# Deltanet then MLP-mixer on one core: 1999 steps of a hand-kept order of work permuted

## The chip, the cores and the metric

The kernel runs on one core of a Trainium2 chip. The core has five engines with an instruction queue each: TensorE (PE in the profile, its weight loads apart as PEld), VectorE (DVE), ScalarE (ACT), GpSimd (POOL) and SyncE (SP), which here issues every transfer between HBM and the core's memory. The metric is device time in microseconds (us), lower is better. Times are medians of several executions; one execution is taken with the hardware profiler and gives the profile and the trace.

## The reference

Two blocks follow one another. The first is a linear-attention recurrence (delta rule) over 768 tokens for 4 batch items of 8 heads of 48 elements; the second an MLP-mixer with a token part (768 to 256 to 768) and a channel part (384 to 1536 to 384), which takes the first block's output with the heads side by side.

```python
k_n = k / (np.linalg.norm(k, axis=-1, keepdims=True) + 1e-06)
for t in range(S):
    kt, vt, bt = (k_n[:, :, t], v[:, :, t], beta[:, :, t, None])
    y[:, :, t] = np.einsum('bhd,bhde->bhe', q[:, :, t], state)
    v_old = np.einsum('bhde,bhd->bhe', state, kt)
    state = state + bt[:, :, :, None] * np.einsum('bhd,bhe->bhde', kt, vt - v_old)
...
xt = x.transpose(0, 2, 1)
h = np.maximum(xt @ w_tok1, 0.0) @ w_tok2
u = x + h.transpose(0, 2, 1)
h2 = np.maximum(u @ w_ch1, 0.0) @ w_ch2
return (u + h2).astype(np.float32)
```

## The kernel before, in words

**Chunks, units, batches.** The recurrence is done in chunks of 64 tokens: 12 chunks to a batch item, 48 in all (`recur`, r0 to r47). What a chunk needs besides the state is made ahead for a unit of two chunks (128 tokens of one batch item, all 8 heads; u0 to u23): its k and q rows, their turned form, the products of k and q within a chunk, and the inverse of a triangular matrix for each head. When the 12 chunks of a batch item are through, its mixer (m0 to m3) can run.

**Jobs.** Each piece of work is a Python generator, and each `yield` in it ends a step. The jobs, named by a letter and a number:
- `k` loads k and q (L385). From unit 12 on, `load_rows` (L359) brings the k rows in four transfers into a tile called `pads`, `stacked` (L403) brings k once more into `kst`, and `load_rows` brings the q rows in four.
- `p` (prep) turns the rows with VectorE transposes (`turn_rows`, L368) and makes norms and scales. `c` and `d` (`grams`) are the products within the unit's two chunks: matmuls into `p_g` (L442), then a VectorE product with a mask into `gm` (L445).
- `t` (`to_parts`, L612) writes 32-row blocks of `gm` to a buffer in HBM called `n_dram`; `i` (`invert`) reads the blocks of several units as one tile `x` and inverts them on VectorE in a round of some thirty steps, each a product into `sub` (L676) and an addition to `x` (L680); `f` (`from_parts`, L637) brings the blocks back from `w_dram`. The first two rounds (units 0 to 5) stay on the chip and need no such transfers; round 2 holds units 6 to 9, round 4 units 14 to 17, round 5 units 18 to 21. `h` and `j` (`join_16`, `join`) put larger inverses together from the blocks.
- `v` loads v of a unit into `v_st` (four transfers, L403) and scales it on GpSimd (L416).
- `r` is a chunk of the recurrence: matmuls with the state (L813), the subtraction of `v_st` (L820), two more groups of products, the new state `s_t` (VectorE, L860) and the output rows, copied into `xb`, the mixer's input.
- `m` is a mixer. Its token part has the products `p` (L1009) and `p_h` (L1022); `p_h` is added into `xb` by VectorE (L1026), six times. Then the rows are turned on PE (transposes, copied by ScalarE at L1036 into `u_t`), and the channel part follows for pairs of 128 tokens: `p_c` (L1089) in the first mixer, a scheme with fewer products (L981 to L997) in the others, combinations on VectorE (L1063), and seven products `p_o` (L1111), each added into `xb` by VectorE (L1040).
- `w` rounds the mixer's weights from 64-bit input (ScalarE, VectorE at L282, GpSimd at L286) and makes differences of some (VectorE, L301); `s` makes weight sums (VectorE, L922); `b` loads beta. `x`, `z`, `y` and `Y` are filler matmuls on zeros (L227, L237), which only keep PE at work.

**PSUM.** The mixer's products share three PSUM banks (L101, `bufs=3`), taken in turn: the fourth group has to wait until the first group's bank has been read. Two banks each serve the recurrence and the preparation.

**The order of the work.** `manual_schedule` is on, so nothing reorders instructions: each engine runs its instructions in the order in which the program issues them, and waits where a semaphore says so. That order is a table at the end of the kernel function, a string of 2740 steps. A loop takes the words one after another and moves the named job on by one step:

```python
for word in order.split():
    name, _, n = word.partition("*")
    for _ in range(int(n or 1)):
        next(jobs[name])
```

`k13*4 r14` thus issues four steps of unit 13's load (here four transfers on SP) and then one step of chunk 14. One step can put instructions on several queues.

Of the kernel before, what the change touches and what calls it, by code (L numbers as in the profile page):

```python
# [23 lines left out]
def kernel(  # L24
# [149 lines left out]
    t11 = const.tile([128, NB, HB], FP32, name="t11")  # L174
# [18 lines left out]
    w1 = const.tile([128, NCH, DTOK], FP32, name="w1")  # L193
# [998 lines left out]
    p6 w8 v0 i0*2 k8 p4 i0 w1 i0*2 p6 p4*3 c4 w1 i0 w17 w1 c4*4 x i0*2 p5 z k7 w8
    k8 i0*2 z i0 k8 w6 k8 i0*3 x z v1 z k8 z d4 x d4 w17 d4 w6 d4 z h0 d4 w17 t4
    h0*4 i0 h1 w0 f0 k8 h1 f0 p6 h1 p3 h1 f0 h1 z w8 k7 f1*3 h0*4 h2*2 h0*4 k7*2
    h2*2 v1 h2 p5 w8 w11 w0 z f2 j0 f2 j0*5 w0 h1*2 f2 h1*3 j0 h1 v0 h1*2 w6 j0*3
    p5 j1 p5*2 t4 p5 w0 h2 j0 p5 h2 p5*3 h2*2 r0*2 w6 h2 r0*2 h2*2 r0 h2 c5*4 w14
    r0*2 d5 w11 d5*2 c5 w11*2 r0 r1*4 w14 d5 r1 d5 p6 t5 r1 j1*3 r1 k9 j1 w9 r1 k7
    p6 k10 h3*3 w14 t5*2 j1*2 h3 p8 j1 j2 j1*2 r1 r2*3 t4 i1 r2 r1 i1 h3 j2 f3*2 x
    r2 j1 w9 p6 v2*4 w16 w14 j2 v2 f3 j2 k9 r2 i1 k9 r2 p8 j2 p6 i1 j2 i1 r2 p7
    h3*2 r2 p6 r2 h3 d6 k9*3 h3 p6 d6 i1*2 d6*2 r3*2 k7 w27 h3*2 r3*2 h3*2 p8 k10  # L1200
    c6 i1 w9 c6 r3*2 c6 w9 k10 w16 d6 i1 v3 c6 w16 r3 j2 k10 j2 r3 c6 j2 j3 r3
    r4*2 j2 v3 r4 p7 r4 p8 j3 w16 i1 r3 p7 j3 v3 j3 t6 r4 j3 j2 i1 p9 w24 p7 r4*2
    j3 p7*2 k10 i1 r4 p7 v3 p7*2 w5 r4 p7 t6*2 r4 r5*4 i1 c7 w27 r5 d7 c7 v4 i1 c7
    d7 k11 c7 r5 v3 i1 r5 d7 c7 d7 v4 w5 r5 d7 p8 j3 r5 p8 w5 w24 j3 r6*2 i1 w27
    w5 r6*2 p8 j3*2 w24 p9 w27 p8 r6 p8 t7 x z h5*3 w26 t7 j3 h5 r5 h4 t7 v4 t7 h4
    r6 w24 i1 t6 h5 p9 h4*2 r6 c8*2 h4 v4 w28 r6 c8 f4*2 p9 d8 c8 r6 w7 c8 f4 d8*4
    h4 r7*2 h4*2 r6 r7*2 w26 h4*2 w26 r7 h4 p9 v4 h4 t8 j4 h4 w26 p9 r7 t8 p9*2
    r7*3 p9 w28 c9*2 d9 c9 f5 c9 r8*2 d9 r8 w28 d9 c9 t8 f5*2 w7 d9 j4 w4 d9 w28
    w27 t8 p8 v5 r8 v5 p10 j4*3 m0 j4 p10 j4 w27 j4*2 w7 p10 w15 j4 r7 h5 r8 j4 w4
    t9*2 h5*2 w27 p10 h5 r8 w4 r8 z t9 w7 r8 w15 h5*2 w15 t9 r8 r9 h5 p9 k10 v5 r8  # L1210
    r9*2 w4 j5 r9*2 h5 p10 v5 w15 i2 r9 j5*2 p10 r9*2 w19 r9 v5 Y j5 i2*4 p10 j5 x
    j5 r10 i2 j5*2 r10 w29 p10*2 r9 k12 i2 Y i2 r10*2 j5 k12 j5 k11 w12 r10 k11
    k12 k11*2 z j5 w19 Y c10 r10 i2 Y i2*2 r10*2 w29 k12 w12 d10 w29 i2 d10 m0
    k12*2 r10 i2 k12 r11 w12 k12 r11*2 c10 r11 i2 d10 p11 r10 k11 w12 r11 w22 x*2
    p11 w29 i2 v6 i2 w19 k12 w19 i2 z w22 i2 v6*2 m0 k12 i2 v7*2 r11 w22 r11 v6
    w22 w25 m0*2 w21 k12*2 c10 r11 d10 r11 c10 p12 p11 m0 i2*6 m0 w31 i2 m0 i2*4
    w21 i2*2 v7 w25 w31 m0*2 f6 c10 m0*2 f6*2 p11 w31 m0 w31 m0 f6 f7*3 s p12 w21
    f7 p11 s d10 v6 p11 p10 j6 p12 w25 f8*2 m0 w25 f8*2 w21 m0*2 j6*3 p12 j6*2 m0
    j7*6 j8 m0 r12*5 w23*2 w20 j8 w29 j8 r12 v7 f9 j8 w25 f9*2 r12 j8 r13*2 r12
    r13 w30 j8 p11 w23 s r13 t10*2 r13 w23 p12 v8 m0 v8 k13 w32 r13 p11 r13*3 k13  # L1220
    p11 c11 w23 c11 k13 w20 d11 w30 w29 c11 v8 d11 c11 w20 c11 w30 v7 d11 r14 t10
    r13 w25 w32 d11 r14 w30 r14 j9 d11 k13*4 r14 w20 p12 k13 p12 r14 m0 w32 m0*2
    k13*2 m0 k13 r14 c12 w32 r14 t11 d12 v8 c12 d12 c12 p11 p13 t11 d12*2 r14 k13
    r14 d12 p12 m0 r15 v8 c12 p13*2 r15*4 m0 c12 t10 w33 r14 r15 f9 p13 t12 p13*3
    m0 t11 m0*2 d13 t12 t11 c13 r15 d13 c13 t12 d13 c13 d13 k14*2 w33*2 c13 r15*2
    d13 c13 m0 k14 m0 k14*2 w33 k14*2 s w31 w33 m0 w23 r16 k14 t13 j9 r16 t13*2 j9
    r16 j9 r16 w33 t12 r16 w29 j9 r15 m0*2 t13 j9 w31 r16 w31 v9 m0 p14*2 r16 w23
    r16 k14*2 r16 m0 r17 w25 i3 j9 w33 r17 p14 j9 p13 k14 v9 r17 j9 p14 r17 p14
    r17 v10 k15*3 v10 r16 m0*2 i3*3 k15 m0*3 k15 i3 v10 k14 k15 r17 i3 v9*2 r17
    i3*4 k15 i3 m0 p14 i3*2 r17*3 m0*2 p14 k15 i3*2 m0*2 v9 p14 m0*2 i3*4 m0 i3*2  # L1230
    k15*2 r18 d14 k15 r18*2 p15 d14 r18*2 j9 m0 i3 k15 i3 p15 i3*2 j9 p15 i3*7
# [36 lines left out]
    j18 t23 m1 j19*4 i6 m1 j19 f21*2 m1*4 r36*4 m1 r35 i6*4 m1 j20 m1 f19 f20 i6
    r36 i6 r36 i6 r36 i6 m2*2 i6*2 m1 r37*3 r36 r37 i6 r37 i6 m2*3 i6 r37*2 v19*3
# [48 lines left out]
```

## Time and profile before

| | before |
|---|---|
| median of 3 runs | 646.3 us |
| the runs | 644.84, 646.3, 648.53 us |
| profiled execution | 642.82 us |
| its span on the core | 641.0 us |
| mean granted TensorE clock | 0.987 |
| bytes read from / written to HBM | 39.42 / 9.44 MB |

The profiled execution is 3.5 us below the median of the runs and 2.0 below the fastest. Its span is the time from the first to the last instruction; some 1.8 us lie around it. In the tables by stage, a stretch has the busy time of PE, PEld, DVE, ACT and POOL with the count of instructions in brackets, then the granted TensorE clock, the mean busy share of the DMA engines and GB/s. In a timeline row stand the start, the duration, the engine, the line, the operation, the tile written and the tiles read, the count, and in square brackets the idle time of that engine just before with what ended it. SPq is SP's queue: its rows are the issues of transfers, not the transfers themselves.

### The profile page before, as it was taken

The page shows a single profiled execution, that of the slowest core. Times are in us where ns is not written, and L with a number is a line of the kernel's source. Part 1 is how long each engine was busy: PE and PEld are TensorE (multiplying, and loading weights), DVE is VectorE, ACT ScalarE, POOL GpSimd, SP SyncE. Part 2 cuts the span into 40 slices and gives each one's busy share as a digit, 9 for nine tenths or more (in the row PEclk, how much of TensorE's full clock was granted, in tenths as well). Part 3 has the DMA queues.
Part 4 walks back from the last instruction along what each step waited for, and adds up shares of the span by engine and source line. Part 5 has one row for each costly group of instructions (what it writes and reads, how often), then busy time and mean ns, then how long its engine had stood idle before and what let it go on. Part 6 is the DMA issues. An engine that isn't in the chain of part 4 may idle for free.

```text
span 641.0 us, 21509 instructions
## 1 busy us (share of the span) xinstructions
PE 613.8 (96%) x9136; PEld 531.7 (83%) x9136; DVE 443.0 (69%) x1132; ACT 260.4 (41%) x631; POOL 108.9 (17%) x147
## 2 busy tenths in 40 slices
PE   7499899999999999999989999999999999999997
PEld 4358786568898988959989999769999987999997
DVE  4885877987879568987958998784727253373643
ACT  7749787446413232125513424044334131132240
POOL 2446354243310122021121001000100000000000
PEclk9889899999999999999989999999999999999999
DMA  9785667546552454244442223203010000000000
GB/s 170 164 173 123 146 156 199 140 96 155 112 127 60 82 114 102 67 119 80 96 100 69 63 69 55 59 7 56 4 41 2 27 2 0 26 1 26 2 26 26
DMA packets 135776, 50.27 MB, mean 78 GB/s; under 512 B 114656, under 2 KB 130144, under 8 KB 135680
## 3 DMA queue, kind: packets, MB, share of 16 engines
q1 hardware_dynamic: 135680, 48.89, 34.3%
q8 instruction: 72, 1.18, 0.8%
q14 instruction: 24, 0.20, 0.1%
HBM read 39.42 MB, written 9.44 MB: 76 GB/s over the span
## 4 chain that ended last, share of the span: by engine, by line
PE 79%; DVE 7%; ACT 5%; DMA 3%; SPq 3%; issue 2%; POOL 0%; DVEq 0%; ACTq 0%; POOLq 0%
PE p_o L1111 25%; PE p_r L981 19%; PE p_c L1089 7%; PE p_h L1022 4%; PE p L1009 4%; PE p_g L442 3%; PE p_k L813 2%; PE p_s L851 2%; PE p_y L833 2%; PE p_z L773 2%; DVE sub L676 2%; SPq L403 2%; DVE x L680 2%; PE p_warm L227 2%; PE p_w L837 1%
## 5 line engine op out<-in xcount | busy, mean ns | idle before, releaser
L1111 PE MATMUL p_o<-wc,r 128*128 128x192 f32 x720 | 128.7, 331 | 0.6 <-ACT u_t L1036 0.6
L1111 PEld LDWEIGHTS p_o<-wc,r 128*128 128x128 f32 x720 | 117.6, 191 | 3.0 <-ACT u_t L1036 1.1
L993 DVE TENSOR_TENSOR r<-r,p_r 128x512 f32<-128x512 f32 x90 | 60.0, 685 | 49.0 <-PE p_r L981 48.1
L990 ACT COPY r<-p_r 128x512 f32<-128x512 f32 x54 | 31.6, 585 | 94.2 <-PE p_r L981 87.2
L1040 DVE TENSOR_TENSOR xb<-xb,p_o 128x192 f32<-128x192 f32 x84 | 29.4, 350 | 57.1 <-PE p_o L1111 56.7
L680 DVE TENSOR_TENSOR x<-x,sub 128x84 f32<-128x84 f32 (+24 forms) x178 | 61.2, 344 | 6.1
L676 DVE TENSOR_TENSOR sub<-x 128x84 f32<-128x84 f32 (+24 forms) x178 | 57.8, 325 | 5.8 <-DMA x<-n_dram 1.9
L416 POOL TENSOR_TENSOR v_st<-v_st,nrm 128x384 f32<-128x384 f32 x24 | 20.8, 866 | 180.2 <-DMA v_st<-in_v_dram 134.0
L1111 PE MATMUL p_o<-wc,s 128*128 128x192 f32 x288 | 50.7, 330 | 0.3 <-DVE xb L1040 0.3
L1089 PE MATMUL p_c<-u_t,wc 128*128 128x256 f32 x216 | 50.5, 386 | 0.2 <-ACT u_t L1036 0.2
L442 PE MATMUL p_g<-kq 48*64 48x128 f32 (+1 forms) x704 | 38.9, 284 | 12.3 <-ACT kq L511 9.1
L1111 PEld LDWEIGHTS p_o<-wc,s 128*128 128x128 f32 x288 | 46.7, 190 | 1.2 <-DVE xb L1040 0.6
L997 ACT ACTIVATE r<-r 128x512 f32<-128x512 f32 x54 | 33.8, 630 | 28.5 <-DVE r L993 28.2
L1089 PEld LDWEIGHTS p_c<-u_t,wc 128*128 128x128 f32 x216 | 39.9, 190 | 5.9 <-ACT u_t L1036 0.4
L865 ACT ACTIVATE xb<-p_y 64x192 f32<-64x192 f32 x96 | 31.2, 325 | 26.0 <-DMA out_dram<-xb 9.5
L442 PEld LDWEIGHTS p_g<-kq 48*64 48x64 f32 (+1 forms) x704 | 27.8, 136 | 16.4 <-ACT kq L511 11.0
L843 ACT COPY w_t<-p_w 128x192 f32<-128x192 f32 x48 | 15.2, 317 | 61.6 <-PE p_w L837 60.4
L981 PE MATMUL p_r<-u_t,wc 128*128 128x128 f32 x288 | 38.5, 277 | 0.0
L499 POOL TENSOR_TENSOR mb<-mask_c,cs 128x512 f32<-128x512 f32 x20 | 21.0, 1049 | 99.0 <-DVE gm L445 72.2
L981 PE MATMUL p_r<-t_d,wc 128*128 128x128 f32 x288 | 37.4, 280 | 0.0
L981 PEld LDWEIGHTS p_r<-u_t,wc 128*128 128x128 f32 x288 | 35.4, 192 | 0.3
L286 POOL TENSOR_TENSOR wc<-w_f,d 128x384 uint32<-128x384 uint32 x24 | 25.2, 1057 | 59.3 <-DVE w_f L282 28.8
(176 smaller groups left out, 1252.7 us busy)
## 6 DMA issues: line engine op xcount, KB each, us to landing
d<-in_moe_w_ch_dram SPq DMA_DIRECT2D x24, 384.0 KB, 3.8
v_st<-in_v_dram SPq DMA_DIRECT2D x96, 48.0 KB, 2.4
out_dram<-xb SPq DMA_DIRECT2D x23, 192.0 KB, 1.9
kst<-in_k_dram SPq DMA_DIRECT2D x64, 48.0 KB, 2.7
n_dram<-gm SPq DMA_DIRECT2D x72, 32.0 KB, 2.0
pads<-in_k_dram SPq DMA_DIRECT2D x24, 96.0 KB, 3.1
pads<-in_q_dram SPq DMA_DIRECT2D x24, 96.0 KB, 2.5
gm<-w_dram SPq DMA_DIRECT2D x72, 32.0 KB, 2.0
```

What stands on the lines that cost most here:

```text
L442: nc.tensor.matmul(p_g[PAR[i ^ cc], p], kqt[f, p, cc, 0], kqt[f, p, cc])
L676: nc.vector.tensor_tensor(out=tmp, in0=col.to_broadcast(dims), in1=row.to_broadcast(dims), op=ALU.mult,)
L680: nc.vector.tensor_tensor(out=new, in0=new, in1=tmp, op=ALU.add)
L865: nc.scalar.mul(y[:, :, D * i : D * i + D], p_y[PAR[1 - i]], 1.0 if c else -1.0)
L981: nc.tensor.matmul(p[:, i], pieces[i // width][:, at : at + 128], f[f"u{n}"], start=first and i == 0, stop=True, skip_group_check=True,)
L990: nc.scalar.copy(o, p)
L993: nc.vector.tensor_tensor(out=o, in0=o, in1=p, op=ALU.add if sign > 0 else ALU.subtract)
L997: nc.scalar.activation(o, o, ACTF.Relu)
L1009: nc.tensor.matmul(p_1[dh], piece_of(w1, c, 0)[:, dh * 128 : (dh + 1) * 128], xb[:, c], start=(c == 0), stop=(c == NCH - 1),)
L1040: nc.vector.tensor_tensor(out=xb[:, c, e], in0=xb[:, c, e], in1=p, op=ALU.add)
L1089: nc.tensor.matmul(p_c[:, k], piece_of(wc1, cb, f * 128)[:, f * 128 : (f + 1) * 128], u_t[:, cb], start=(cb == 0), stop=(cb == NCB - 1),)
L1111: nc.tensor.matmul(p, a[:, m], wc2[:, m, j], start=(start and i == 0), stop=(i == NM - 1), skip_group_check=True,)
```

## The change

The diff has one hunk: the table. Its first 1999 steps stand in another order; each step occurs as often as before, the fillers too, and each job's own steps keep their order. The last 741 steps are the same. No instruction is added, removed or altered, no tile or buffer has another size. Places that change hands between jobs (PSUM banks, buffers) are taken in the new order.

```diff
-    z*4 w10*3 k1 k0 w10 b k0 k1*5 p1*2 k0*3 k3 k0 b p0 w2 p1 k2 b v1 p0*4 x k2 k3
...
+    z*4 w10*4 x k1 k0 b k1*3 k0 k1*2 k0 p1 k0*2 p1 b w2 k0 p0*2 p1 v0 b p0 v0 p0*2
...
```

What it does is seen in the queues of the engines. Three places follow, in the order in which the prediction takes them up.

SyncE's queue where unit 21's q rows are loaded (about 320 us in the trace). `pads_92<-in_q_dram` are those rows, in four transfers; `v_st_4871` (before) and `v_st_4884` (after) are the v rows of unit 16; `n_dram` takes blocks to round 5 of the inversion, and `w_dram` is where blocks of round 4 come back from. Before:

```order
L403 DMA kst1_94<-in_k_dram 64x4x48 x4
L359 DMA pads_92<-in_q_dram 32x4x192
L359 DMA pads_92<-in_q_dram 32x4x160
L359 DMA pads_92<-in_q_dram 32x4x192
L612 DMA n_dram_4732<-gm_96 32x8x32
L403 DMA v_st_4871<-in_v_dram 64x4x48 x2
L612 DMA n_dram_4732<-gm_96 32x8x32 x2
L359 DMA pads_92<-in_q_dram 32x4x160
L637 DMA gm_96<-w_dram_4419 32x8x32
```

After:

```order
L403 DMA kst1_94<-in_k_dram 64x4x48 x3
L359 DMA pads_92<-in_q_dram 32x4x192
L359 DMA pads_92<-in_q_dram 32x4x160
L359 DMA pads_92<-in_q_dram 32x4x192
L359 DMA pads_92<-in_q_dram 32x4x160
L612 DMA n_dram_4812<-gm_96 32x8x32 x4
L637 DMA gm_96<-w_dram_4408 32x8x32
L612 DMA n_dram_4812<-gm_96 32x8x32
L637 DMA gm_96<-w_dram_4408 32x8x32
L612 DMA n_dram_4812<-gm_96 32x8x32 x2
L637 DMA gm_96<-w_dram_4408 32x8x32
L359 DMA pads_92<-in_k_dram 32x4x192
```

The fourth q transfer has moved up behind the third, ahead of the three `n_dram` and two `v_st` transfers; the two `v_st` transfers stand three rows further down than the last row shown, behind the first k rows of unit 22 and two more `n_dram` transfers.

VectorE's queue where the first mixer adds its token products (about 129 us). The rows of L676 and L680 are steps of round 2 of the inversion, counted by the last number of the x row (24x7, 25x6 and so on); L1026 are the adds that free the mixer's banks. Before:

```order
L676 TENSOR_TENSOR sub<-x 128x168
L680 TENSOR_TENSOR x<-x,sub 128x24x7
L1026 TENSOR_TENSOR xb<-xb,p_h 128x384
L676 TENSOR_TENSOR sub<-x 128x150
L680 TENSOR_TENSOR x<-x,sub 128x25x6
L1026 TENSOR_TENSOR xb<-xb,p_h 128x384
L676 TENSOR_TENSOR sub<-x 128x130
L680 TENSOR_TENSOR x<-x,sub 128x26x5
L676 TENSOR_TENSOR sub<-x 128x108
L680 TENSOR_TENSOR x<-x,sub 128x27x4
```

After:

```order
L676 TENSOR_TENSOR sub<-x 128x150
L680 TENSOR_TENSOR x<-x,sub 128x25x6
L676 TENSOR_TENSOR sub<-x 128x130
L680 TENSOR_TENSOR x<-x,sub 128x26x5
L676 TENSOR_TENSOR sub<-x 128x108
L680 TENSOR_TENSOR x<-x,sub 128x27x4
L1026 TENSOR_TENSOR xb<-xb,p_h 128x384
L676 TENSOR_TENSOR sub<-x 128x84
L680 TENSOR_TENSOR x<-x,sub 128x28x3
L1026 TENSOR_TENSOR xb<-xb,p_h 128x384
```

The first two adds stand three steps of the inversion later. A mask product `gm<-p_g,mb` (L445), which before stood behind the fourth add, now stands eight steps ahead of the first, behind the step 19x12.

VectorE's queue in the first mixer's channel part (about 170 us). L1063 are combinations for the products, L1040 is the add that frees a bank, L301 are weight differences, L922 a weight sum. Before:

```order
L368 STREAM_TRANSPOSE kq_99<-pads 128x4x4x32 x2
L1063 TENSOR_TENSOR s_2721<-r_2411 128x384
L1063 TENSOR_TENSOR s_2722<-s_2721,r_2411 128x384
L1063 TENSOR_TENSOR r_2411<-r_2411 128x3x128
L282 TENSOR_SCALAR w_f<-d_2833 128x384
L860 TENSOR_TENSOR s_t_113<-s_t_114,p_s 128x192
L445 TENSOR_TENSOR gm<-p_g,mb 128x4x128 x2
L1040 TENSOR_TENSOR xb<-xb,p_o 128x192
L922 TENSOR_TENSOR lent<-wc_126,lent 128x512
L301 TENSOR_TENSOR wc_127<-wc_127 128x192 x6
```

After:

```order
L301 TENSOR_TENSOR wc_127<-wc_127 128x192 x2
L860 TENSOR_TENSOR s_t_113<-s_t_114,p_s 128x192
L301 TENSOR_TENSOR wc_127<-wc_127 128x192 x3
L445 TENSOR_TENSOR gm<-p_g,mb 128x4x128 x2
L282 TENSOR_SCALAR w_f<-d_2831 128x384
L1063 TENSOR_TENSOR s_2721<-r_2404 128x384
L1063 TENSOR_TENSOR s_2722<-s_2721,r_2404 128x384
L1063 TENSOR_TENSOR r_2404<-r_2404 128x3x128
L1040 TENSOR_TENSOR xb<-xb,p_o 128x192
L301 TENSOR_TENSOR wc_127<-wc_127 128x192 x3
```

Six of the weight differences (one of them between the two transposes ahead of the rows shown) now stand ahead of the combinations and of the add, where six stood behind it before.

More of the change, by code (lines that the diff above doesn't have):

```diff
@@ L1192 @@
[L1192 to L1219, printed above, removed]
@@ L1276 @@
[L1276 to L1280 removed]
+    z*4 w10*4 x k1 k0 b k1*3 k0 k1*2 k0 p1 k0*2 p1 b w2 k0 p0*2 p1 v0 b p0 v0 p0*2
+    k3 p0 p1 z p0*2 k2 p1 k3 p0 c0*2 w2 p1 d0*2 k2 k4 d0 c0 w2 p0 k3 c0*2 d0 w13
@@ new lines @@
+    w7 c9 j4*2 f5 r8*2 j4 f5 r8 j4 w27 w15 p10 r8 r7 t9*2 w4 w27*2 t9 m0 j4*2 t9
+    j4 w4 h5 j4*2 z k10 w15 r8 v5 h5 v5 r8 w7 w4 w15 h5*3 i2 h5*2 w15 r8*2 j5 w19
+    k11 p9 Y h5 r8 r9*4 k11 r9 p10 r9 w12 x r9*2 p10 r9 w7 w29 v6 j5*4 Y i2*2
+    r10*3 j5*2 r10 i2 v5 i2 r10 j5*2 i2 r9 j5 z j5 r10 w19 r10 i2 w19 i2*2 r10*2
+    p10*3 k12 i2 d10 r11 r10 w29 r11 k11*2 w12 i2 k11*2 d10 c10 k12 i2 d10 k12
+    r11*2 Y m0 r11 i2 w12 v7 w12 i2 p11 Y r11*2 p11 v7*2 w22 v7 x d10 r11 w22 w19
+    i2*2 w29 i2 m0 i2*2 w21 w22 v6 k12 i2 d10 v6 i2 k12*6 i2 c10 x c10*2 z r11 i2
@@ new lines @@
+    k13 d12 r14 c12 d12 c12 p13 w32 d12 c12 r15*2 v8 r15 d12 t11 w23 k13 t11 d12
+    p13*2 p12 c12 r15 j9 m0 c12 m0 w33 r15 p13*3 m0 w23 r15 t11 r15 m0 t12 p13 r15
+    t11 w31 r15 t12*2 w31 k14*3 w31 c13 k14 d13 c13 d13 t12 c13 k14*2 d13 k14 w25
+    v8 c13 d13*2 c13 w33*2 r16 m0 k14 m0 w33 m0 w23 m0*2 r16 j9*2 r16 j9 r16 w33
+    r16 j9 r15 m0 t13*3 j9 t13 s p13 w33 p14 k14*2 p14 m0 w33 j9 r16 m0 r16 i3
+    r16*2 m0 k14 r17 p14*2 j9 r17 j9 r17 v10*2 j9 r17 p14 m0 i3 k15 i3 r17 i3
+    k15*2 m0 i3*3 m0 v10 m0 r16 i3 m0 r17 k15 p14 k14 i3 r17 i3 v9*4 m0 i3 k15 v9
@@ new lines @@
+    r29 p20 r29 k20 r29 k20*2 m1*2 v15 p20 c19 k21*3 r28 r29 m1*4 r29 v15 p20 r29
+    m1 v16 m1 v15 p20 k21 m1 r29 m1*2 k21 r29 v16 m1 k21*2 r29 m1*2 k21*2 p20 r30
+    j16 r30 j16 r30 k21*3 m1*2 j16 r30*2 t19*3 m1 j16*2 m1 c20 r30 c20 p21*2 d20
+    c20*2 r30 d20 r30 d20 p21 d20 t19 c20 f17 t18 r30 r31 p21 r31 d20 r31*3 r30
+    p21 f17 t20 m1 p21 r31 t20 r31 m1 f16 m1 k22 t20 r31 p21 c21 r31 t20 m1 d21
+    c21 j17 d21 c21 d21 r32 d21*2 c21 r32 m1 c21 m1*2 r32 v16*2 m1*3 t21*4 m1
+    k22*3 m1*3 i5 r32 k22 j17*5 m1 v18 m1*3 k22*3 v16 r32 r31 i5 p22 i5*3 m1*2
@@ L1281 @@
+    m2*2 m3*2 m2 m3*3 m2*2 m3 m2 m3*7 m2 m3*4 m2*4 m3 m2 m3*2 m2*7 m3*154
     """
```

136 lines of the change are left out of this document (70 added, 66 removed).

## The prediction

> **What bounds the kernel now.** I read the page's shares and slices first, then the table by stage, then the waits of the matrix engine, and went from there to the places where it stood still.
>
> ```profile
> span 641.0 us, 21509 instructions
> PE 613.8 (96%) x9136; PEld 531.7 (83%) x9136; DVE 443.0 (69%) x1132; ACT 260.4 (41%) x631; POOL 108.9 (17%) x147
> PE   7499899999999999999989999999999999999997
> PEclk9889899999999999999989999999999999999999
> ```
>
> TensorE (PE) is busy for 96% of the span, and the clock row shows the few dips below full speed: three early slices, and one at about 325 us. Nothing else is near its limit over the whole span. So time can only be gained where PE stands still or is slowed.
>
> ```profile
> 0.00:40.00 40.00, 26.83 (x260) 17.70 (x261) 28.85 (x89) 27.02 (x68) 13.37 (x24) 0.87 0.98 176
> 40.00:106.90 66.90, 62.57 (x1742) 50.50 (x1744) 47.15 (x118) 54.37 (x147) 38.05 (x48) 0.97 0.63 150
> 106.90:136.80 29.90, 27.87 (x325) 17.47 (x318) 27.95 (x81) 14.37 (x36) 4.33 (x4) 1.00 0.58 145
> 136.80:355.00 218.20, 214.43 (x3641) 187.38 (x3642) 172.00 (x427) 78.95 (x201) 44.65 (x57) 0.99 0.44 98
> 355.00:641.00 286.00, 282.11 (x3183) 258.67 (x3182) 167.04 (x420) 85.67 (x180) 8.48 (x14) 1.00 0.11 26
> ```
>
> The columns are the stretch, its length, then busy time of PE, its weight loads, VectorE (DVE), ScalarE (ACT) and GpSimd, the granted clock, DMA share and GB/s. The last 286 us are PE's: 3.9 us idle, full clock. From 136.8 us on PE is the bound, with 3.8 us idle in 218. Between 106.9 and 136.8 VectorE is as full as PE (27.95 of 29.90). Only before 106.9 does PE idle much: 13.2 and 4.3 us, in a web of short steps on all engines.
>
> **What the change can reach.** The last 741 of the 2740 steps are the same in both tables, and they begin at about 355 us. Both tables hold the same steps in the same numbers, the filler matmuls too. So what changes is idle time and slow clock before 355 us, and the end moves by as much as PE's work is brought forward or pushed back there. I looked at the steps ahead of each early milestone (the first inversion, the first chunk of the recurrence, the mixer's first matmul). The sums differ by about 1 us of an engine's work either way, up to 106.9 us, so I put that stretch at nothing. It isn't a proof: no row shows what those 17.5 us of idling would do in another order, and a gain or a loss of 2 us there is held in the range.
>
> **The transfer at 320 us.** The clearest stall after 136.8 us:
>
> ```profile
> 317.21 0.43 SPq L612 DMA_DIRECT2D n_dram<-gm  x1
> 317.69 1.26 SPq L403 DMA_DIRECT2D v_st<-in_v_dram  x2
> 318.99 1.09 SPq L612 DMA_DIRECT2D n_dram<-gm  x2
> 320.13 3.11 DMA pads<-in_q_dram
> 321.04 1.12 DVE L368 STREAM_TRANSPOSE kq<-pads 128x512 f32<-128x512 f32 x1
> 323.32 1.10 DVE L368 STREAM_TRANSPOSE kq<-pads 128x512 f32<-128x512 f32 x1 [1.17 <-DMA pads<-in_q_dram]
> 324.48 0.67 PE L442 MATMUL p_g<-kq 48*64 48x128 f32 x16 [1.49 <-DVE kq L368]
> 331.97 0.36 DVE L820 TENSOR_TENSOR rest<-p_k,v_st 128x192 f32<-128x192 f32 x1
> ```
>
> The fourth row is from the chain of waits, the others from the timeline (start, duration, work, in brackets the wait ahead). The last quarter of unit 21's q rows is issued at 320.13 and lands 3.11 us later. VectorE, done with the k transpose at 322.16, waits 1.17 us for it, and PE waits 1.49 us for the transpose. In the changed queue of SyncE the five issues of the first three rows (two `v_st`, three `n_dram`) stand behind that transfer. They take 2.9 us here. Some 0.7 us of other issues has come ahead of it earlier in the queue, so it goes out 2.2 to 2.9 us sooner and lands by 320.3 to 321.0, ahead of 322.16. VectorE then starts the q transpose at once: **-1.2 us**. Next late is VectorE itself, so about 0.3 of PE's 1.49 us stays. Two transfers of `v_st` (unit 16) now go out some 9 us later; their reader is the subtraction of chunk 32 in the last row (331.97), so about 1 us of margin is left.
>
> The clock belongs to the same stall:
>
> ```profile
> 72.46:75.87 3.41, 2.11 (x88) 2.00 (x88) 2.84 (x12) 2.32 (x7) 0.70 (x1) 1.00 0.43 85
> 75.87:79.28 3.41, 3.41 (x56) 2.57 (x48) 2.09 (x6) 1.67 (x5) 1.99 (x3) 0.50 0.74 164
> 130.49:133.90 3.41, 2.32 (x8) 1.04 (x6) 3.10 (x14) 1.51 (x4) 0.00 (x0) 1.00 0.00 0
> 321.63:325.04 3.41, 1.46 (x68) 1.22 (x63) 2.15 (x4) 0.97 (x3) 3.04 (x6) 1.00 0.42 72
> 325.04:328.45 3.41, 3.41 (x38) 3.32 (x33) 2.09 (x6) 0.00 (x0) 0.00 (x0) 0.50 0.35 64
> ```
>
> Each half-speed stretch (clock 0.50) is a piece of 3.41 us, and the piece ahead of it held 1.46 or 2.11 us of PE work. A piece with 2.32 us (130.49) cost nothing. So the limit lies between 2.11 and 2.32 us of 3.41. With 1.17 us less waiting the piece before 325.04 holds about 2.6, above it, so the slow piece goes. PE is the bound there, and half speed for 3.41 us is worth **-1.7 us**; where the piece is slow all the same, 0. The Trainium skill ("TensorE: Matmul & The Clock Gate", Part 1) gives the same 3413 ns window and the two speeds; its rule of thumb is that a PE gap has to exceed about 3.4 us to bring half speed. The trace speaks against that length: the longest gap ahead of 325.04 is 1.49 us. By the rule, this slow piece would have nothing to do with the stall, and the sum below would be without the 1.7.
>
> **The same pattern, unit 17.**
>
> ```profile
> 238.18 1.26 SPq L403 DMA_DIRECT2D v_st<-in_v_dram  x2
> 240.14 0.59 SPq L403 DMA_DIRECT2D v_st<-in_v_dram  x1
> 243.97 1.10 DVE L368 STREAM_TRANSPOSE kq<-pads 128x512 f32<-128x512 f32 x1 [1.25 <-DMA pads<-in_q_dram]
> 245.12 1.10 PE L442 MATMUL p_g<-kq 48*64 48x128 f32 x32 [0.57 <-DVE kq L368]
> ```
>
> The three `v_st` issues (1.85 us) go behind the last q rows here as well, but about 1.5 us of others come ahead. The transfer gains some 0.4 us of a PE wait of 0.57: **-0.3 us**, between 0 and -0.6.
>
> **VectorE at the mixer's adds, 129 us.** Here the change pushes back.
>
> ```profile
> 126.09 6.72 PE L1022 MATMUL p_h<-r,w 128*128 128x384 f32 x20
> 129.14 0.55 DVE L1026 TENSOR_TENSOR xb<-xb,p_h 128x384 f32<-128x384 f32 x1
> 130.18 0.55 DVE L1026 TENSOR_TENSOR xb<-xb,p_h 128x384 f32<-128x384 f32 x1
> 133.37 0.52 DVE L1026 TENSOR_TENSOR xb<-xb,p_h 128x384 f32<-128x384 f32 x1
> 133.94 1.56 PE L1022 MATMUL p_h<-r,w 128*128 128x384 f32 x4 [1.13 <-DVE xb L1026]
> 136.78 2.42 PE L1089 MATMUL p_c<-u_t,wc 128*128 128x256 f32 x10 [0.19 <-ACT u_t L1036]
> L445 DVE TENSOR_TENSOR gm<-p_g,mb 128x512 f32<-128x512 f32 x44 | 29.6, 684 | 3.4 <-PE p_g L442 3.0 <-DMA pads<-in_q_dram 0.2
> ```
>
> Six groups of four `p_h` matmuls (about 1.3 us each) share three PSUM banks, so the fourth needs the first add, the fifth the second, the sixth the third. Between the second add's end (130.73) and the third (133.37) stand five steps of inversion round 2: 0.53 us a step. In the changed order three more such steps and one `gm` product (0.68) stand ahead of the first add: 3 x 0.53 + 0.68 = 2.3 us. VectorE has next to no idle time to take that up, so the first add ends at 132.0 instead of 129.7. PE, done with three groups at 130.0 and with a group of transposes (0.6) that now follows them, waits until then; three groups of 1.3 end at 135.9 instead of 135.5. The copies and `p_c` follow as before, with one more 0.6 us group of transposes taken ahead of `p_c`, which is work saved later. The last add stands 1.7 us later, which would let `p_c` start at about 138.0 instead of 136.8. Between 135.9's +0.4 and that +1.2, less 0.6 saved, I take **+0.6 us**, with 0 as the lower end. The upper end is 1.2 without the saving, and 2.9 if the wait of 1.5 to 2 us falls into one clock piece: 3.41 less 1.5 to 2 lies below the limit of 2.11 to 2.32.
>
> **VectorE at 170 us.**
>
> ```profile
> 160.00:164.00 4.00, 4.00 (x64) 3.02 (x54) 3.03 (x10) 2.18 (x6) 2.75 (x4) 1.00 0.50 108
> 164.00:168.00 4.00, 4.00 (x78) 3.56 (x81) 3.37 (x5) 1.15 (x3) 1.83 (x2) 1.00 0.83 174
> 168.00:172.00 4.00, 4.00 (x135) 3.72 (x128) 3.96 (x10) 2.48 (x7) 1.81 (x2) 1.00 0.40 97
> L301 DVE TENSOR_TENSOR wc<-wc 128x192 f32<-128x192 f32 x24 | 8.8, 385 | 0.5
> ```
>
> Six weight differences (L301, 0.385 us each, 2.3 us) have moved ahead of the mixer's add of about 170 us, which frees a bank. VectorE idles 1.6 us between 160 and 168, so the add is late by 0.7 us, by 0 if more idle time lies in reach, by 2.3 if none does. `p_o` has three banks too, and a product's length of slack. I take **+0.5 us**, 0 and 2.3 as ends, and 1.7 on top of that if it costs a clock piece.
>
> **The sum.** -1.2 - 1.7 - 0.3 + 0.6 + 0.5 = -2.1 us. The profiled execution took 642.8 us with its span of 641.0; it would be 640.7. The median of the runs shown is 646.3 (644.84 to 648.53), 3.5 us above the profiled one; I take the same difference from it: **644.2 us**. A measurement of this kernel can tell about 0.5% (3.2 us) from no change, so faster means under 643.1, slower over 649.5. The forecast is no change that can be told, -0.3%.
>
> **The rivals.** *Faster, 641.4 us.* Both VectorE delays fall into idle time (their 1.1 us is not paid) and the slow piece at 75.87 us goes as well (-1.7 at most): -1.2 - 1.7 - 0.3 - 1.7 = -4.9. For it: that piece held 2.11 us of PE work, just under the limit, so a little filling is enough. Against it: in the changed order PE has the products that covered its wait for the state of chunk 4 ahead of the step that starts that wait. Chance 0.32.
>
> *The slow clock piece at 325 us stays, 645.9 us.* It would be set by something other than the stall, or its place in time shifts onto other idle time. Then only -1.2 - 0.3 + 1.1 = -0.4 is left. For it: only two such pieces and the long early one are there to learn the limit from. Against it: each of them follows a piece of little work. The Trainium skill's rule above would bring this case about. Chance 0.08.
>
> *Slower, 650.0 us.* VectorE's queue is the mechanism: adds that free PE's banks stand behind work moved ahead of them, at 129 us at the price of 2.9, and at 170 us at the price of 2.3 + 1.7 = 4.0, against 3.2 gained: +3.7. For it: VectorE is 93% full from 106.9 to 136.8 us and full at 168 to 172, so what is put ahead is paid. Against it: PE has three banks, and PE's own order was shifted along in both places. From 3.2 us of such waits on it is no gain, from 6.4 on slower by 0.5%. Chance 0.20.
>
> That the change does not do what it says is no rival here: the order of the instructions shows the moves.
>
> **How the numbers follow.** Forecast 0.40, with its own range of 642.3 (no VectorE delay, and half a microsecond less idling early) to 645.9, of which 0.06 lies under 643.1. Faster 0.32 + 0.06 = 0.38; within 0.5% 0.34 + 0.08 = 0.42; slower 0.20. The range of eight in ten is 639.0 to 650.0: the faster case less 2.4 for the early stretch, which no row prices, and the slower case at its price.
>
> **What would show it.** Right: in the changed profile VectorE's second transpose of unit 21 starts with no DMA wait behind the first, and the clock is 1.00 there; the `p_h` matmuls show one wait of 1.5 us or more for the adds of L1026, with the first `p_c` at 137 to 138 us. Wrong: a clock piece of 0.50 after 136.8 us, a wait of PE over 1 us for a transfer, or a start of the mixer's `p_c` more than 2 us away from 136.8.

## The result, and the profile after

The changed kernel took 642.59 us (median of 20 runs, 639.26 to 647.26), the kernel before 646.24 us (20 runs, 642.53 to 649.68): a ratio of 0.9947, 95% interval 0.9927 to 0.9967. A second series on another chip gave 0.9917 (0.9883 to 0.9951). The prediction said 644.2 us from 646.3, that is -2.1; measured are -3.4 us by the ratio (-4.7 to -2.1 by the interval) and -5.4 (-7.6 to -3.2).

The first trace of the changed kernel is its slowest run, 647.26 us, and that of before was a short one, 642.82 us; so a second trace of each was taken. A half-speed piece, or slow piece, is below one of the 3.41 us at a granted clock of 0.50 that the prediction describes. First the table by stage of that slowest run, in the columns used before:

```profile
0.00:40.00 40.00, 27.45 (x262) 18.20 (x263) 29.83 (x89) 27.43 (x68) 13.92 (x24) 0.91 0.97 180
40.00:106.90 66.90, 60.37 (x1691) 49.30 (x1689) 45.36 (x118) 53.18 (x147) 36.64 (x47) 0.97 0.60 138
106.90:136.80 29.90, 27.33 (x341) 17.94 (x342) 23.24 (x65) 12.14 (x31) 5.49 (x6) 0.83 0.60 149
136.80:355.00 218.20, 214.93 (x3559) 185.06 (x3561) 174.45 (x438) 80.52 (x205) 42.37 (x53) 1.00 0.45 98
355.00:645.50 290.50, 286.62 (x3298) 262.88 (x3292) 170.18 (x426) 87.42 (x183) 11.03 (x18) 1.00 0.11 27
```

Against before, the clock is now 1.00 from 136.8 us on (0.99 before) and 0.83 between 106.9 and 136.8 (1.00 before). What this run lost lies early: a half-speed piece at 87.57 us and three in a row from 111.46 us.

```profile
87.57:90.98 3.41, 3.41 (x74) 3.41 (x72) 1.38 (x4) 3.08 (x8) 1.74 (x3) 0.50 0.45 122
111.46:114.88 3.42, 3.24 (x44) 1.51 (x36) 3.00 (x10) 1.78 (x5) 0.00 (x0) 0.50 0.60 113
114.88:118.29 3.41, 2.42 (x39) 1.93 (x41) 1.80 (x6) 1.15 (x3) 0.00 (x0) 0.50 0.17 45
118.29:121.70 3.41, 3.41 (x42) 2.78 (x41) 1.95 (x6) 2.52 (x7) 0.00 (x0) 0.50 0.00 0
323.09:326.50 3.41, 2.90 (x108) 2.41 (x107) 3.34 (x11) 2.51 (x8) 0.00 (x0) 1.00 0.49 109
326.50:329.91 3.41, 3.41 (x92) 2.91 (x91) 3.10 (x5) 1.15 (x4) 1.20 (x2) 1.00 0.25 39
```

The last two pieces are unit 21's. Where the piece before held 1.46 us of PE work, it now holds 2.90, and the one behind it runs at full clock. SyncE's and VectorE's timeline of the same trace shows why:

```profile
321.36 3.03 SPq L359 DMA_DIRECT2D pads<-in_q_dram  x4
324.44 1.92 SPq L612 DMA_DIRECT2D n_dram<-gm  x4
327.18 1.10 DVE L368 STREAM_TRANSPOSE kq<-pads 128x512 f32<-128x512 f32 x1
328.64 1.14 DVE L368 STREAM_TRANSPOSE kq<-pads 128x512 f32<-128x512 f32 x1 [0.18 <-PE p_w L837]
```

All four q transfers are issued in a row, and the second transpose waits for no transfer. At the p_h adds (129 us before) the second trace of the changed kernel, a run with a span of 637.2 us, has:

```profile
130.05 0.55 DVE L1026 TENSOR_TENSOR xb<-xb,p_h 128x384 f32<-128x384 f32 x1
132.33 0.52 DVE L1026 TENSOR_TENSOR xb<-xb,p_h 128x384 f32<-128x384 f32 x1
125.41 4.14 PE L1022 MATMUL p_h<-r,w 128*128 128x384 f32 x12
130.66 4.14 PE L1022 MATMUL p_h<-r,w 128*128 128x384 f32 x12 [0.68 <-DVE xb L1026]
136.07 3.29 PE L1089 MATMUL p_c<-u_t,wc 128*128 128x256 f32 x14 [0.19 <-ACT u_t L1036]
```

The wait stands ahead of the fourth group instead of the sixth and is 0.68 us instead of 1.13. The first add (130.05) starts 4.6 us behind the first p_h, where it was 3.1 before; the third (132.33) starts 6.9 us behind it, where it was 7.3. From the first p_h to the first p_c are 10.7 us, as before (126.09 to 136.78).

**How runs of one kernel differ.** Over all series the mean granted clock was 0.986 for before (87 runs, 0.981 to 0.995) and 0.990 for the changed kernel (32 runs, 0.984 to 0.995). One half-speed piece lowers it by 0.0027 (3.41 x 0.5 / 641), so before has 5.3 of them in a mean run, the changed kernel 3.7. Within one kernel, each 0.0027 goes with 1.2 us of span (136 runs of eleven series of changed orders and repeats, correlation -0.71; the 87 runs of before alone give -0.55). The pieces begin at another place in every trace (28.09 and 28.31 us in two of before, 29.54 and 27.30 in two of the changed kernel). The Trainium skill ("TensorE: Matmul & The Clock Gate", Part 1) says that the window is free-running and does not start anew with a kernel; the traces agree.

### The profile page after: what moved, and what is told of

It is laid out like the page before. It is cut to its first block, busy times and chain, and to the rows that moved or that the text cites. A ratio compares the mean times of both kernels' runs of the same rounds, so it can differ in the third digit from the quotient of the medians.

```text
span 645.5 us, 21499 instructions
## 1 busy us (share of the span) xinstructions
PE 616.7 (96%) x9136; PEld 533.4 (83%) x9136; DVE 443.1 (69%) x1132; ACT 260.7 (40%) x631; POOL 109.5 (17%) x147
## 4 chain that ended last, share of the span: by engine, by line
PE 82%; ACT 7%; DMA 3%; DVE 3%; issue 1%; SPq 1%; POOL 1%; ACTq 0%; DVEq 0%
PE p_o L1111 25%; PE p_r L981 20%; PE p_c L1089 6%; PE p_h L1022 5%; PE p L1009 5%; PE p_g L442 4%; PE p_k L813 3%; PE p_y L833 3%; PE p_s L851 3%; PE p_z L773 2%; PE p_warm L227 2%; DMA d<-in_moe_w_ch_dram 2%; PE p_ut L1032 1%; PE p_y L852 1%; PE p_w L837 1%
## 5 line engine op out<-in xcount | busy, mean ns | idle before, releaser
L1040 DVE TENSOR_TENSOR xb<-xb,p_o 128x192 f32<-128x192 f32 x84 | 29.4, 350 | 61.0 <-PE p_o L1111 60.5
L676 DVE TENSOR_TENSOR sub<-x 128x84 f32<-128x84 f32 (+24 forms) x178 | 58.7, 330 | 8.9 <-DMA x<-n_dram 5.0
L680 DVE TENSOR_TENSOR x<-x,sub 128x84 f32<-128x84 f32 (+24 forms) x178 | 58.7, 330 | 6.1
```

The costliest lines, as they stand in the source:

```text
L676: nc.vector.tensor_tensor(out=tmp, in0=col.to_broadcast(dims), in1=row.to_broadcast(dims), op=ALU.mult,)
L680: nc.vector.tensor_tensor(out=new, in0=new, in1=tmp, op=ALU.add)
```

## The experiments

All are the kernel before or the changed one with another order of the table, so nothing is left out of the computation. Two series of the unaltered kernels come first.

**e1, the kernel before again.**

> The kernel before, unaltered, to learn how its runs differ among themselves. In the 20 runs of the changed kernel the mean granted clock lay between 0.984 and 0.995 and the span followed it; one half-speed piece of 3.41 us lowers the mean clock of a 641 us span by 0.0027. Theory A (the prediction: fixed stalls; the pieces of the profile, five of them, belong to the program) expects a clock of 0.986 to 0.988 in nearly every run, spread of spans under 2 us. Theory B (how many pieces fall to half speed differs from run to run, since the 3.41 us grid begins at another place of the program each time) expects clocks from about 0.978 to 0.990, with a median span near 644.4 at about 6 pieces (clock 0.984), some 1.4 us per piece.

Measured: ratio 1.0008 (0.9977 to 1.004), spans 640.6 to 650.8 in 12 runs, clocks 0.979 to 0.995. Theory B holds: pieces and time differ from run to run. Its trace has two slow pieces behind unit 21's wait, where the first trace had one:

```profile
325.27:328.68 3.41, 1.54 (x66) 1.25 (x64) 2.03 (x3) 1.44 (x4) 3.33 (x5) 1.00 0.34 60
328.68:332.10 3.42, 3.14 (x46) 3.05 (x47) 1.55 (x5) 0.00 (x0) 0.34 (x2) 0.50 0.49 89
332.10:335.51 3.41, 3.41 (x13) 3.41 (x12) 2.87 (x12) 0.00 (x0) 0.00 (x0) 0.50 0.29 45
```

**e2, the changed kernel again.**

> The changed kernel, unaltered, for a second trace of it: the first one was its slowest run (647.26 us against a median of 642.59). Ratio to before 0.993 to 0.997 by every theory. Theory A expects in the trace no PE wait over 1 us for unit 21's q rows, one wait of 1.5 us or more for a p_h add near 129 us, and p_c at 137 to 138 us, with one half-speed piece fewer than before on average. Theory B expects the wait for the p_h adds only if no half-speed piece comes shortly ahead of it, and two pieces fewer than before on average (about 4 against 6).

Measured: 0.9917 (0.9883 to 0.9951); 3.5 pieces per run. No wait for unit 21's rows; the p_h wait is 0.68 us where theory A had 1.5 or more.

**e3 and e4, the early part alone and the late part alone.** The table's steps ahead of chunk 12 (931 steps of before) and those behind, each once in the new order:

```diff
 e3
-steps of before ahead of r12, old order
+the same steps, in the order of the changed table
 steps from r12 on, old order
 e4
 steps of before ahead of r12, old order
-steps from r12 on, old order
+the same steps, in the order of the changed table
```

> The changed order for the steps that before does ahead of chunk 12 (to about 146 us), the old order behind them. Theory A expects what the prediction gives the early part: +0.6 us for the p_h adds and nothing else, 646.2 to 647.5 us. Theory B expects that most of the gain is here, since all early half-speed pieces lie here: -2 to -3 us, 643 to 644.5 us, mean clock higher by 0.003 to 0.005 than that of before, and the stall at 320 us with its piece still there.

> The old order for the steps ahead of chunk 12 (to about 146 us), the changed order behind them. Theory A expects -1.2 - 1.7 - 0.3 + 0.5 = -2.7 us, 643.5 us, with the stall for unit 21's q rows gone from the trace. Theory B expects -0.5 to -1.5 us (the stall and its piece, in the share of runs in which the piece falls to half speed), 644.7 to 645.7 us, with as many early pieces as before.

Measured: early 1.0010 (0.9983 to 1.0037) with 5.5 pieces, late 0.9951 (0.9930 to 0.9972, -3.2 us) with 3.8 pieces. The gain is in the late part, as theory A had it; theory B's early gain is not there. That the late part also takes 1.5 pieces from a run is B's point. The two halves together make -2.5 us, where e2 in the same series has -5.4; with intervals of 2 us either way, whether they add up stays open.

**e5, one step of the kernel before moved.** SyncE's queue:

```diff
 L359 DMA pads<-in_q_dram 32x4x192
+L359 DMA pads<-in_q_dram 32x4x160
 L612 DMA n_dram<-gm 32x8x32
 L403 DMA v_st<-in_v_dram 64x4x48 x2
 L612 DMA n_dram<-gm 32x8x32 x2
-L359 DMA pads<-in_q_dram 32x4x160
```

> The kernel before with one step moved: the last of unit 21's q transfers goes right behind the third, ahead of the three n_dram and two v_st transfers; nothing else differs. Theory A (the late transfer makes the gain of the late part, which was 3.1 us in mean span): -1.2 - 1.7 = -2.9 us, mean span 641.6, no PE wait over 1 us in front of unit 21's products. Theory B (the wait itself is nearly free, what it costs is half-speed pieces): -1.5 to -3 us, with 1 to 1.4 pieces fewer per run than the 5.2 of before. Theory C (the gain of the late part is spread over many places): -1 us or less, 4.5 to 5 pieces.

Measured: 0.9972 (0.9939 to 1.0006), -1.8 us, 4.1 pieces where before has 5.4 in the same series. The pieces are those of theory B; the time, -3.9 to +0.4 us by its interval, rules out none of the three. The wait for unit 21's rows is gone from the trace. The same trace shows what else there is, at unit 17, which this edit leaves as it was:

```profile
244.75 1.10 DVE L368 STREAM_TRANSPOSE kq<-pads 128x512 f32<-128x512 f32 x1
247.88 1.09 DVE L368 STREAM_TRANSPOSE kq<-pads 128x512 f32<-128x512 f32 x1 [2.03 <-DMA pads<-in_q_dram]
249.03 1.10 PE L442 MATMUL p_g<-kq 48*64 48x128 f32 x32 [1.75 <-DVE kq L368]
```

VectorE waits 2.03 us and PE 1.75, where the first trace of before had 1.25 and 0.57, and a slow piece follows:

```profile
246.83:250.24 3.41, 1.67 (x45) 1.26 (x45) 2.32 (x4) 0.00 (x0) 2.02 (x4) 1.00 0.39 62
250.24:253.66 3.42, 3.42 (x19) 2.79 (x16) 3.33 (x7) 0.00 (x0) 0.00 (x0) 0.50 0.57 101
```

**e6, the wait filled.** One filler ahead of unit 21's first product:

```diff
-r31*2 c21 d21
+r31*2 z c21 d21
```

> The kernel before with one filler matmul (128x512, about 1.04 us) added on TensorE right ahead of unit 21's first product, where it waits about 1.5 us for the transpose of the late rows. The transfer stays late and the wait stays as long, it is only filled. If the wait costs time by itself: 0 us. If it costs by the half-speed pieces behind it (theory B): -1 to -2.5 us, 1 to 1.4 pieces fewer per run, clock 1.00 at 320 to 335 us in the trace.

Measured: 0.9984 (0.9951 to 1.0016), 4.2 pieces, again 1.2 fewer than before; the time doesn't tell. The trace does for one run: the transpose waits 1.68 us, PE runs the filler and waits another 0.92, and no slow piece follows.

```profile
326.20 1.09 DVE L368 STREAM_TRANSPOSE kq<-pads 128x512 f32<-128x512 f32 x1 [1.68 <-DMA pads<-in_q_dram]
325.30 1.12 PE L227 MATMUL p_warm<-warm 128*128 128x512 f32 x2
327.34 0.67 PE L442 MATMUL p_g<-kq 48*64 48x128 f32 x16 [0.92 <-DVE kq L368]
```

The stretch around it (step 30 to step 100 of the second mixer) takes 55.0 us against 53.6 without the wait, so in this run the wait costs 1.4 us by itself.

**e7, two other waits of the changed kernel taken away.** Its first trace has two places where a step that waits for a transfer stands ahead of work that does not need it. VectorE and PE at 260 us, and ScalarE at 81 us:

```profile
263.74 0.19 DVE L676 TENSOR_TENSOR sub<-x 128x30 f32<-128x30 f32 x1 [2.88 <-DMA x<-n_dram]
264.58 0.35 DVE L1040 TENSOR_TENSOR xb<-xb,p_o 128x192 f32<-128x192 f32 x1
264.99 1.24 PE L1111 MATMUL p_o<-wc,s 128*128 128x192 f32 x6 [1.86 <-DVE xb L1040]
81.21 0.56 ACT L279 ACTIVATE d<-d 128x384 f32<-128x384 f32 x1 [1.46 <-DMA d<-in_moe_w_ch_dram]
82.11 0.71 ACT L687 ACTIVATE r<-r,odd 128x512 f32<-128x512 f32 x1
```

Two inversion steps, which wait for x, stand ahead of the add that frees PE's bank; a rounding of weights stands ahead of the copy that round 1 of the inversion needs. In the trace of e2 the same x step waits 0.82 us and PE not at all.

```profile
255.00 0.19 DVE L676 TENSOR_TENSOR sub<-x 128x30 f32<-128x30 f32 x1 [0.82 <-DMA x<-n_dram]
```

```diff
-s i4 m0 i4 m0 i4
+s m0*2 i4*3
-w24 i1 v4 j3 w5
+i1 v4 j3 w24 w5
```

> The changed kernel with two places mended where its trace shows VectorE or ScalarE waiting for a transfer that others queue behind: the mixer's product and add near 260 us goes ahead of the two inversion steps that wait for x from n_dram (PE waited 1.9 us there), and the rounding of weight piece 24 on ScalarE goes behind the copy of inversion round 1 (ScalarE waited 1.46 us near 81 us, PE then 1.6 us). If these waits cost: -0.5 to -2.5 us against the changed kernel (mean span 640.3), its slowest runs gone, no PE wait for xb over 0.5 us at 255 to 265 us. If they are made good by later idle time: 0 +- 0.5 us.

Measured: 0.9956 (0.9918 to 0.9994). In its trace neither step waits for a transfer any more, and it is not faster than the changed kernel. They come in some runs; what they cost in a mean run is below what this measures.

**e8, the stall put back into the changed kernel.**

```diff
 L359 DMA pads<-in_q_dram 32x4x192
-L359 DMA pads<-in_q_dram 32x4x160
+L612 DMA n_dram<-gm 32x8x32 x3
+L403 DMA v_st<-in_v_dram 64x4x48 x2
+L359 DMA pads<-in_q_dram 32x4x160
```

> The changed kernel with the late transfer put back: two v_st transfers and the last of unit 21's q transfers stand behind three n_dram transfers again, as in the kernel before; all else as changed. Theory A: +2.9 us against the changed kernel (mean span 640.3, so 643.2), the PE wait of 1 to 1.7 us for unit 21's transpose back in the trace. Theory B: +1.5 to +3 us, with 1 to 1.4 half-speed pieces more than its 3.7. Theory C: under +1 us.

Measured: 0.9951 (0.9918 to 0.9983), that is -3.2 us from before, where the changed kernel had -3.4 and -5.4: 0 to +2 us, which with the width of the intervals rules out neither nothing nor theory A's 2.9. Its pieces are 3.6 per run, no more than the changed kernel's 3.7: those that theory B expected to come back did not. The wait is back in the trace, without a slow piece:

```profile
322.57 0.87 PE L1032 MATMUL p_ut<-ident,xb 128*128 128x128 f32 x6
323.99 1.09 DVE L368 STREAM_TRANSPOSE kq<-pads 128x512 f32<-128x512 f32 x1 [1.47 <-PE p_ut L1032]
325.14 0.89 PE L442 MATMUL p_g<-kq 48*64 48x128 f32 x24 [1.08 <-DVE kq L368]
```

The bracket names a group of PE transposes, but that group ends at 323.44; the last q transfer, issued at 320.91, lands at 323.91, just ahead of the VectorE transpose. The stretch from step 30 to step 100 takes 55.3 us instead of 53.6.

**e9 and e10, unit 17's transfers alone, and both units'.**

```diff
 L359 DMA pads<-in_q_dram 32x4x192
 L359 DMA pads<-in_q_dram 32x4x160
-L403 DMA v_st<-in_v_dram 64x4x48 x2
-L359 DMA pads<-in_q_dram 32x4x192
-L403 DMA v_st<-in_v_dram 64x4x48
-L359 DMA pads<-in_q_dram 32x4x160
+L359 DMA pads<-in_q_dram 32x4x192
+L359 DMA pads<-in_q_dram 32x4x160
+L403 DMA v_st<-in_v_dram 64x4x48 x3
```

> The kernel before with two steps moved: the third and fourth of unit 17's q transfers go right behind the second, ahead of the three v_st transfers (about 240 us). Prediction's term for it: -0.3 us (0 to -0.6), mean span 644.4. Theory D (that term was read from one trace with a short wait; four other traces of the old order show VectorE waiting 1.5 to 2.0 us there, twice with a half-speed piece behind it): -1.5 to -2.5 us, mean span 642.2 to 643.2, no PE wait over 0.4 us in front of unit 17's products, and the stretch from the mixer's step 60 to its step 80 at 37.3 us instead of 38.3 to 40.6.

> The kernel before with both q transfers moved, unit 17's and unit 21's; nothing else differs. If these two transfers are the gain of the late part: -3 to -4 us, mean span 640.7 to 641.7, 3.5 to 4 pieces, no faster than the kernel with the whole late part changed (641.4). If the rest of the late part carries it: -1.5 to -2 us, as unit 21 alone.

Measured: unit 17 alone 0.9997 (0.9968 to 1.0026), both 0.9932 (0.9900 to 0.9965), -4.4 us with 4.0 pieces. Both transposes of each unit now run in one piece, and PE is busy for 217.24 of the 218.20 us between 136.8 and 355 (214.43 in the first trace of before, 3.8 us idle):

```profile
238.51 2.05 DVE L368 STREAM_TRANSPOSE kq<-pads 128x512 f32<-128x512 f32 x2
317.60 2.04 DVE L368 STREAM_TRANSPOSE kq<-pads 128x512 f32<-128x512 f32 x2
136.80:355.00 218.20, 217.24 (x3695) 190.16 (x3696) 175.42 (x434) 82.24 (x207) 42.89 (x55) 1.00 0.46 100
```

Within the intervals, three steps moved give what 1999 gave. That unit 17 alone shows no gain in its runs while its trace shows the shorter stretch (37.3 us) stays open; its interval reaches to -2.1 us.

**The two places in all traces.** VectorE's wait for the last q rows, and the length of a stretch around it, with steps counted from 0. For unit 17 it runs from PE's first work of step 60 of the first mixer to VectorE's combination (L1063) of step 80, which in the old order stands right behind the late transpose; for unit 21 from PE's work of step 30 of the second mixer to that of step 100.

| order at the place | unit 17: wait, stretch (us) | unit 21: wait, stretch (us) |
|---|---|---|
| old: before | 1.25, 38.3 | 1.17, 56.2 (1 slow piece) |
| old: e1 | 1.56, 39.4 | 1.38, 58.2 (2) |
| old: e3 | 1.95, 39.8 | 0.35, 53.7 |
| old: e5, e6 (unit 17) | 2.03, 40.6; 2.09, 40.1 (1 slow piece right behind each) | |
| old: e9 (unit 21) | | 1.02, 56.1 (1) |
| old: e11 | none, 37.5 | 1.14, 54.5 |
| old: e12 | 2.29, 39.6 | 2.20, 57.5 (1) |
| new, seven traces (unit 21: six) | none, 37.3 to 37.5 | none or 0.18, 53.1 to 53.9 |

The means of the old order are 39.3 and 56.0 us, of the new one 37.3 and 53.6: 2.0 us at unit 17 (without the two slow pieces behind its stretch), 2.4 at unit 21 (with its slow pieces). Measured on PE, up to its next p_c, unit 17's stretch is 41.1 us in the old order and 39.4 in the new one, so 1.7 us there. The two places together are thus worth 4.1 to 4.4 us in the traces; e10 has 4.4 (2.3 to 6.5 by its interval). Between 136.8 and 355 us each of the eight traces of the old late part (before, e1, e3, e6, e11 and e12, and e5 and e9 with one place moved) has one or two slow pieces, nine in all, five of them at unit 21 and two at unit 17; the five traces of the changed late part (the first, e2, e4, e7, e8) and that of e10 have none.

The wait differs so in part because the transfer does: unit 17's last q transfer was issued at 240.66 and landed at 244.46 in e6 (3.8 us), at 243.44 and 246.00 in e11 (2.6 us), in the same queue order. The rest is VectorE's: it was done with the transpose ahead 1.9 us behind that issue in e6 and 3.0 us in e11.

**e11 and e12, the p_h adds in the kernel before made late.**

```diff
 e11
-m0 w31 i2 m0 i2*4 w21
+w31 i2*3 m0 i2 m0 i2 w21
 e12
-m0 w31 i2 m0 i2*4 w21 i2*2
+w31 i2*5 w21 i2*2 m0*2
```

> The kernel before with the first two p_h products and their adds three inversion steps later, where the changed kernel has them (about 129 us); one look, read by the stretch from the first of these p_h products to the first p_c, 10.7 us in three traces of before and 10.7 in three of the changed order. Prediction's term: +0.6 us (0 to 2.9), so 11.3 us. Theory that the third add decides and does not move: 10.7 +- 0.2 us.

> The kernel before with the first two p_h products and their adds behind the last step of inversion round 2, 2.6 us or more behind their old place; one look, the same stretch. By the reckoning of the prediction (each step ahead of an add is paid, 0.53 us): first p_h to first p_c does not shrink, and p_c starts about 2 us later against r11, the chunk before. If the third add decides: p_c starts no later than in before, since the third and fourth adds keep their place.

Measured: in e11 the first p_h starts at 127.73 and the first p_c at 138.75, 11.0 us against 10.7; the wait in front of the fourth group is 1.47 us, and the one ahead of the sixth is gone.

```profile
127.73 4.14 PE L1022 MATMUL p_h<-r,w 128*128 128x384 f32 x12
133.34 4.14 PE L1022 MATMUL p_h<-r,w 128*128 128x384 f32 x12 [1.47 <-DVE xb L1026]
138.75 3.50 PE L1089 MATMUL p_c<-u_t,wc 128*128 128x256 f32 x15 [0.18 <-ACT u_t L1036]
```

The 0.3 us can't be put down to the adds: e4 and e6, which leave them where before has them, show 10.95 and 11.01 us in their traces. e12 measured something else than was meant (658.08 us, one run). The moved step also issues ScalarE's activations of the token part (L1017), and these now stand behind a weight rounding that waits for its transfer:

```profile
136.42 0.55 ACT L279 ACTIVATE d<-d 128x384 f32<-128x384 f32 x1 [4.38 <-DMA d<-in_moe_w_ch_dram]
137.30 0.85 ACT L1017 ACTIVATE r<-p 128x384 f32<-128x384 f32 x2
137.83 9.63 PE L1022 MATMUL p_h<-r,w 128*128 128x384 f32 x22 [5.16 <-ACT r L1017]
```

PE waits 5.16 us, with two slow pieces behind it (135.6 to 142.4 us). Neither theory is tested by it.

## Why the prediction was right, and where its sum was off

The direction and the mechanism held: the gain is in the late part (e4, -3.2 us), it comes from q transfers that no longer stand behind other transfers (e10, -4.4 us), and the half-speed pieces behind the stall are part of it. The runs with one place changed (e5, e8, e9) are too noisy to price a place by themselves; the prices below are from traces. The size was off: -2.1 us is about half of the -3.4 and -5.4 measured, and the forecast of no change that can be told did not hold to the letter. By the prediction's own line faster begins under 643.1 us, and the median is 642.59; both intervals exclude no change. The forecast, 644.2, and its faster rival, 641.4, are about equally far away. Point by point:

- **Unit 21, -1.2 and -1.7 us.** Measured 2.4 us by the traces, -1.8 by e5's runs, 0 to +2 when put back (e8). The wait itself costs 1.4 to 1.7 us (e6, e8). The slow piece was taken as certain, from a limit of 2.11 to 2.32 us of PE work that the other traces don't bear out (see the end). Of six old-order traces three have one, one has two and two have none: 5 in 6 traces, 1.4 us.
- **Unit 17, -0.3 us. This is the term that was mis-sized.** It was read from one trace in which the wait was 1.25 us for VectorE and 0.57 for PE. Six others of the old order have 0 to 2.29 us for VectorE; for PE the seven are 0.57, 0.88, 1.67, 1.75, 1.81, none and 1.93, mean 1.2 us. By the stretches the mean is worth 1.7 us on PE and 2.0 on VectorE; e9's runs (-0.2 us, -2.1 to +1.7) do not confirm it. The prediction named the pattern but took the one profile's duration as the transfer's duration, though it differs by 1.2 us from run to run in the same order.
- **The p_h adds, +0.6 us, and the p_o add at 170 us, +0.5 us.** Neither is there: 10.7 us before and after for the first. For the second, the stretch from the first p_c to step 60 of the mixer takes 69.1 to 69.3 us in four traces of the changed order (71.1 in e4, which joins the two orders there), against 68.7 to 70.3 in seven of the old that have no slow piece in it. The prediction summed what moved ahead of the first add and carried it on to the last one, 1.7 us. But the third add, for which the sixth group waited before, stands behind the same inversion step in both orders: two steps behind the second add instead of five. Counted from the first p_h it is 0.4 us earlier in e2's trace, and the last add is 0.35 us later (9.80 against 9.45). The wait of 1.5 us or more that was to show the prediction right is 0.68, and p_c starts at 136.07 instead of 137 to 138. e11's 11.0 us lies within what traces without the move show.
- **The early stretch, put at nothing.** e3 confirms it in the mean (1.0010), though single runs differ by the pieces at 76 to 91 and 111 to 122 us.
- **The rivals.** The faster one had it right that VectorE's delays cost nothing, and wrong that early slow pieces go: e3 has 5.5 per run, before 5.3. That the slow piece stays is refuted in the mean: 5.3 against 3.7, and none between 136.8 and 355 us in the traces of the changed late part. VectorE's queue as a brake (the slower one) shows up, but at 260 us and in two traces of the changed late part (1.86 us of PE in the first, 1.11 in e4), not at 129 or 170.
- **What the prediction would have called wrong.** The first trace does show p_c at 142.8 us, 6 us late, and a slow clock behind 106.9. e3 has the same pieces at the same times, in the run whose grid begins at nearly the same place (29.58 against 29.54 us). So it goes with the place of the grid: in e2, p_c starts at 136.07. The order may have a part in it, too: of four traces of the old early part with the grid at nearly that place (e4, e10, e11 and e12, 29.51 to 29.80 us) only e12 has pieces at 87.8 and 111.7 us. That the early part costs nothing is shown by e3's mean alone.

The level of 646.3 for before was right (646.2 to 647.0 in all series), and the first trace, 3.5 us below it, had a shorter wait than most at unit 17 (1.25 us, mean 1.6) and an average one at unit 21 (1.17, mean 1.2).

## What to carry to other kernels

Where an engine waits for a transfer, look at what was issued ahead of it: moving three q transfers ahead of blocks and rows that are needed later was worth as much, within the intervals, as a new order of everything. Take the wait from several traces, since one transfer's time differs by a microsecond and more in the same order, and give it that much room. A stall on a full TensorE is to be priced with the slow clock that follows, by chance and not for certain, and a step that waits for a transfer should not be put ahead of work on its queue that others need.

## What was not expected

Runs of one and the same program spread over 4 to 10 us, and a third to a half of the variance goes with the number of half-speed pieces (correlation -0.55 to -0.71). The amount of PE work in a piece that lets the next one fall to half speed is not one number. Pieces with 1.29 us (e1, 72.7 us), 2.26 us (e3, 84.2 us), 2.41 us (e9, 73.3 us) and even 2.85 us (e12, 5.9 us) were followed by a slow one, while 2.18 us (e2, 109.2 us) and even 1.84 and 1.97 us (the changed kernel, 15.9 and 19.3 us) and 1.56 us (the same, 261.7 us) were not. So the prediction's limit between 2.11 and 2.32 us, read from one trace, is not one, and what else decides stays open.
